# Longformer attention and snake layer on one core: where the next batch's q and k are transposed, when the mask is multiplied in, and which banks hold the scores

## The chip, the cores and the metric

The kernel runs on one core of a Trainium2 chip. The time is device microseconds of one execution; the median of five runs of the kernel before is 370.19 us (369.73 to 371.18). Beside these runs there is one profiled execution, from which all durations below come.

The core has a TensorE (PE in the profile, its weight loads as PEld), a VectorE (DVE), a ScalarE (ACT), a GpSimd (POOL) and a SyncE (SP). Matmuls write to PSUM, which has eight banks of 2 KB per partition; DVE and ACT read them.

## The reference

Two layers follow each other. The first is attention over 8 batches, 8 heads, 576 positions of 64 features, with a window of 32 to both sides and 8 global positions that see and are seen by all. The second is a feed-forward layer over the 4608 tokens with a snake activation.

```python
scores = scale * np.matmul(q, k.transpose(0, 1, 3, 2))
mask = np.abs(pos[:, None] - pos[None, :]) <= window          # window 32
mask = mask | is_global[:, None] | is_global[None, :]
scores = np.where(mask, scores, -1000000000.0)
attn = np.exp(scores - max); attn = attn / (sum + 1e-09)
x = np.matmul(attn, v)        # heads side by side: (4608, 512)
h = x @ w_in                  # (4608, 2048)
s = np.sin(alpha * h)
g = h + s * s / (alpha + 1e-09)
out = g @ w_out               # (4608, 512)
```

## The kernel before, in words

The work is cut into nine phases `p` of a loop at the end of the kernel. Phase `p` (1 to 7) computes the attention of batch `p`, and between its steps it puts the second product of the feed-forward layer (`mm2`) for the 512 tokens of chunk `p-1`. Then it computes the first product and the activation (`mm1`) for chunk `p`. Phase 0 has attention of batch 0 in an order of its own, written out as a string of names; phase 8 has no attention. A chunk needs the batches up to its own number.

The order on every engine is the order in which the program issues instructions (`manual_schedule`). So a line that comes earlier in the text of a step is also earlier in its engine's queue.

**Attention.** Keys and queries of a batch come from memory with positions on partitions (`KS`, `QS`, four transfers of 288 KB, issued by POOL in the first step of the phase before they are used). `stage_T(b, hp)` turns one of four head pairs: 12 transposes of k into the PSUM tile `Kps`, which DVE copies to `kTw[hp]` (L465), and 12 transposes of q into a PSUM tile, which ACT copies to `qT[hp]` (L476). There is one `Kps`, one tile for q at a time, and one `kTw[hp]` and `qT[hp]` for each pair, used by all batches in turn.

The scores are cut into six units `n`. Unit 0 uses pair 0, unit 1 pairs 0 and 1, unit 2 pair 1, unit 3 pair 2, unit 4 pairs 2 and 3, unit 5 pair 3. For a unit, `stage_Q` makes 16 score matmuls into the tile `Sp` (two banks, one buffer, L502), ACT takes the exponential into `E` (L508) and DVE multiplies the mask in (L510). `stage_D` sums over keys with a matmul with ones into `den` (L533); ACT makes 1/sum out of it with a logarithm and an exponential (L539, L541), and DVE sums the global columns (L518, L524). `stage_V` multiplies with the values into `num` (L551), and DVE multiplies with 1/sum into `xT` (L570). `stage_G` (DVE, then eight small POOL copies, L586) writes the global rows of the batch.

`step(j)`, for j from -3 to 5, issues V of unit j, D of unit j+1 and Q, with its mask product, of unit j+3. The function `run` puts `mm2` slots after each step, by the list `counts`. A slot is four matmuls of 128x512; four slots make one output tile of 128 tokens (`ts` 0 to 3), which is then copied to `osb` (L700 on ACT, L698 on DVE for the last tile) and stored. Two slots are issued ahead of step -3. In phases 2 to 7 the third therefore follows step -3, and the fourth, which completes tile 0 and issues its copy, follows step -2.

Pairs 0 and 1 of the next batch are turned in `mm1` (after its slots 10 and 13), pairs 2 and 3 in attention, after steps -2 and 0.

**mm1.** For each of 16 blocks `nt` there are four matmuls into a bank `hb` (L653), a sine on ACT (L660), a square on POOL, ACT or DVE as a table `sq_late` says (L666, L668), and on DVE the sum `H2b = S2 * recip + h` (L643), which frees the bank. That sum is issued two blocks later.

**Banks.** `psC` holds `Kps` and one bank `ops` throughout. The other six banks are `hb` in `mm1` and `num`, `den`, `qp`, `o2`, `Sp` in attention, handed over tile by tile. `Sp` has the two highest banks before the change. The `hb` tiles of `mm1` are given out in the order 2, 7, 6, 5, 4, 3 and then as they come free.

Of the kernel before, what the change touches and what calls it, by code (L numbers as in the profile page):

```python
# [17 lines left out]
def kernel(  # L18
# [11 lines left out]
    nc = tc.nc  # L30
# [442 lines left out]
    def T_Q(b, hp, qpool, qtag, copy):  # L473
        Qps = qpool.tile([P, S], BF, name=qtag)
        T_half(qk[b][0], b, hp, Qps)
        copy(out=qT[hp][:, :, 0:QB], in_=Qps[:].rearrange("p (i c) -> p i c", c=QB))  # L476

    def stage_T(b, hp, pool, tag):
        T_K(b, hp, Kps, nc.vector.tensor_copy)
        T_Q(b, hp, pool, tag, nc.scalar.copy)  # L480

# [15 lines left out]
    def stage_Q(psA, b, n):  # L497
        Sp = psA.tile([P, 2, CH], F32, name="Sp")
        i0 = blocks(n)[0][1]
        for m, (hp, i) in enumerate(blocks(n)):  # L500
            for t, pr in heads:
                nc.tensor.matmul(  # L502
                    out=Sp[:, t, m * QC : (m + 1) * QC],
                    lhsT=kTw[hp][pr, i, :], rhs=qT[hp][pr, i, :],
                    start=True, stop=True, skip_group_check=True,
                )
        E = epool.tile([P, 2, EW], BF, name="E")
        nc.scalar.activation(out=E[:], in_=Sp[:, :, 0:EW], func=AF.Exp, scale=scale)  # L508
        mk = MASK[:, i0 : i0 + NB, :].rearrange("p u c -> p (u c)")
        nc.vector.tensor_tensor(  # L510
            out=E[:], in0=E[:], in1=mk[:, None, :].to_broadcast([P, 2, EW]), op=ALU.mult
        )
        return E

# [78 lines left out]

    def attention(b, psA, t_at=None):


        Es, recs = {}, {}
        gn = gpool.tile([P, 2, NHP, NG], F32, name="gn")
        gd = gpool.tile([P, 2, NHP, NG], F32, name="gd")
        gr = gpool.tile([P, NHP, NG], F32, name="gr")  # L600

        def step(j):
            if j == -3:
                nc.scalar.preload_act_table_set("natural_log_exp_and_others")  # L604
            if j >= 0:
                stage_V(psA, b, j, Es.pop(j), recs.pop(j), gn)
            if 0 <= j + 1 < NUN:
                recs[j + 1] = stage_D(psA, j + 1, Es[j + 1], gd)
                if j + 2 == NUN:
                    stage_Gd(gd, gr)  # L610
                    nc.scalar.preload_act_table_set("trig_and_small")
            if j + 3 < NUN:
                Es[j + 3] = stage_Q(psA, b, j + 3)

        def one(op, j):
            if op == "Q":
                Es[j] = stage_Q(psA, b, j)
            elif op == "D":
                recs[j] = stage_D(psA, j, Es[j], gd)
                if j + 1 == NUN:  # L620
                    stage_Gd(gd, gr)
                    nc.scalar.preload_act_table_set("trig_and_small")
            else:
                stage_V(psA, b, j, Es.pop(j), recs.pop(j), gn)

        if t_at is None:
            return one, partial(stage_G, b, gn, gr)
        parts = [partial(step, j) for j in range(-LEAD, NUN)]
        for hp, j in t_at.items():
            parts[j + LEAD] = partial(chain, parts[j + LEAD], partial(stage_T, b, hp, psA, "qp"))  # L630
        return parts, partial(stage_G, b, gn, gr)

    def chain(*fs):
        for f in fs:
            f()


    def mm1(c, H2b, psB, sq):
# [10 lines left out]
        for nt in range(NT):  # L649
            def slot(nt=nt):  # L650
# [12 lines left out]
                S2 = spool.tile([P, CH], BF, name="S2")  # L663
                eng = sq(nt)
                if eng is nc.scalar:
                    nc.scalar.activation(out=S2[:], in_=Sb[:], func=AF.Square)  # L666
                else:
                    eng.tensor_tensor(out=S2[:], in0=Sb[:], in1=Sb[:], op=ALU.mult)  # L668
# [9 lines left out]
    def mm2(c, H2b, pools, cut=False):  # L678
# [3 lines left out]
        for ts in range(CH // P - (1 if cut else 0)):  # L682
            for g in range(NT // G4):
                def slot(ts=ts, g=g):
# [10 lines left out]
                    if g == NT // G4 - 1:  # L695
                        osb = osbp.tile([P, DM], F32, name="osb")
                        if ts == CH // P - 1:
                            nc.vector.tensor_copy(out=osb[:], in_=ops[:])  # L698
                        else:
                            nc.scalar.copy(out=osb[:], in_=ops[:])  # L700
# [43 lines left out]

    sq_late = lambda nt: {5: nc.scalar, 10: nc.vector, 15: nc.vector}.get(nt, nc.gpsimd)
    sq_last = lambda nt: nc.vector if nt % 4 == 3 or nt > 11 else nc.gpsimd
# [28 lines left out]
    def phase_0():  # L775
        Q, D_, V = (partial(partial, one, o) for o in "QDV")
        fs = {
# [3 lines left out]
        for hp, (kp, ck, qpool, tag) in enumerate(  # L781
            ((Kps, acopy, psA0, "qp"), (Kps0, vcopy, psC, "ops"), (Kps, vcopy, psA0, "qp"), (Kps0, vcopy, psC, "ops"))
        ):
            fs[f"K{hp}"] = partial(T_K, 0, hp, kp, ck)
            fs[f"q{hp}"] = partial(T_Q, 0, hp, qpool, tag, acopy if hp < 3 else vcopy)
            fs[f"G{hp}"] = partial(globals_hp, hp, psA0, "num", vcopy if hp else acopy)
            fs[f"n{hp}"] = partial(globals_in, 1, hp)
        fs["k1"] = partial(globals_hp, 1, psA0, "den", vcopy, (0,))
        fs["p1"] = partial(globals_hp, 1, psA0, "num", vcopy, (1,))
        for o, f in (("Q", Q), ("D", D_), ("V", V)):  # L790
            fs.update({f"{o}{j}": f(j) for j in range(NUN)})
        order = (
            "warm K0 q0 G0 Q0 K1 k1 q1 p1 loads Q1 D0 Q2 D1 K2 q2 G2 D2 Q3 vg K3 q3 G3 D3 Q4 V0 V1 D4 Q5 V2 V3 D5 V4 "
            "alpha V5 last keep A vn kb n0 n1 n2 n3"
# [4 lines left out]
    for p in range(NCH):  # L799
# [4 lines left out]
        elif p < B:  # L804
            with phase_pool("psA", 1) as psA:
                for tag, shape, dt_ in (
                    ("num", [P, NB, QC], F32), ("den", [P, NB, QC], F32),
                    ("qp", [P, S], BF), ("o2", [P, DM], F32),
                ):
                    psA.tile(shape, dt_, name=tag)  # L810
                fill = mm2(p - 1, H2[p - 1], ((psC, "ops"), (psA, "o2")) * 2)
                if p == 1:
                    fill[:8] = [fill[4 * (i % 2) + i // 2] for i in range(8)]
                parts, last = attention(p, psA, {2: -2, 3: 0})
                counts = [1, 1, 1, 1, 1, 2, 2, 1, 0]
                fill.pop(0)()
                fill.pop(0)()
                if p + 1 < B:
# [3 lines left out]
                    for hp in range(NHP):  # L822
                        i_ = hp + LEAD + 1
                        parts[i_] = partial(chain, parts[i_], partial(globals_in, p + 1, hp))
                run(parts + [last], counts + [0], fill)
        else:
# [5 lines left out]
        with phase_pool("psB", 6) as psB:  # L832
# [3 lines left out]
            if p < 3:  # L836
                m1[5] = partial(chain, m1[5], partial(globals_t, p + 1, psB, "hb"))
            if p + 1 < B:
                i_ = (10, 13)
                pre = [partial(shift_v, p + 1), partial(global_v, p + 1)]  # L840
                if p == 0:
                    m1[5] = partial(chain, m1[5], *pre)
                    m1[6] = partial(chain, m1[6], w_loads[3])
                    pre, i_ = (), (12, 14)
                m1[i_[0]] = partial(chain, m1[i_[0]], *pre, partial(stage_T, p + 1, 0, psB, "hb"))
                m1[i_[1]] = partial(chain, m1[i_[1]], partial(stage_T, p + 1, 1, psB, "hb"))
            run(m1, [1, 1, 1, 0] * (NT // 4) if p == B else [0] * NT, fill if p == B else [])
# [33 lines left out]
```

The softmax here doesn't subtract the row's maximum and nothing guards it: scores larger than these inputs give would overflow.

## Time and profile before

| what | value |
|---|---|
| median of five runs | 370.19 us |
| profiled execution, its own time | 369.81 us |
| its span in the profile | 368.0 us |
| PE / DVE / ACT / POOL busy, of the span | 91% / 64% / 67% / 59% |
| from one phase's table load to the next, phases 4 to 7 | 38.18, 38.17, 38.15 us |
| granted PE clock after the first 37 us | 1.00 |

The 1.8 us between the span and the execution's own time lie outside the profile. A phase shows in the profile as a pair of ACT table loads: L604 at the start of attention and L611 near its end. Phases 3 to 7 start within a fraction of a microsecond of the same length, so one of them can be read for all. Times in the timeline are from the start of the span, "idle before" is time in which an engine stood, with the instruction that released it.

### The profile page before, as it was taken

The numbers are of one execution on the slowest core, as the hardware profiler recorded it, in microseconds if no ns is written. First come the engines' busy times: TensorE is split into PE (matmuls) and PEld (weight loads), VectorE is DVE, ScalarE is ACT, GpSimd is POOL, SyncE is SP. The second block draws the span as 40 slices with busy tenths as digits, with TensorE's granted clock in tenths as the row PEclk, the third lists the DMA queues.
The fourth block names the chain that finished last, engine by engine and source line by source line (L and its number), as shares of the span: only waits on it lengthen the run. The fifth ranks groups of instructions, "written<-read, shape, count | busy, mean of one in ns | idle before, by whom it ended". The sixth has DMA issues, their size and how long they took to land.

```text
span 368.0 us, 9350 instructions
## 1 busy us (share of the span) xinstructions
PE 335.9 (91%) x3684; PEld 172.1 (47%) x3738; DVE 234.5 (64%) x511; ACT 248.1 (67%) x378; POOL 217.7 (59%) x316
## 2 busy tenths in 40 slices
PE   5588988999989998999899989998999999999995
PEld 4464444444444444445444454445444544444444
DVE  5565784648763896469746965597649764864610
ACT  3556876768874888487857886678757965845411
POOL 9867798158953895198717881789078005955000
PEclk9557999999999999999999999999999999999999
DMA  9999999941993269642994099509950001001012
GB/s 76 168 197 179 196 175 171 160 117 22 69 175 102 65 39 169 88 109 18 169 110 110 3 160 105 139 0 130 139 137 4 30 30 57 2 0 57 30 66 78
DMA packets 133150, 35.40 MB, mean 96 GB/s; under 512 B 121794, under 2 KB 126818, under 8 KB 133106
## 3 DMA queue, kind: packets, MB, share of 16 engines
q0 software_dynamic: 123120, 20.04, 75.3%
q1 hardware_dynamic: 9682, 14.63, 13.5%
q8 instruction: 29, 0.48, 0.5%
q10 hardware_dynamic: 304, 0.14, 0.1%
q14 instruction: 15, 0.12, 0.1%
HBM read 38.95 MB, written 9.44 MB: 131 GB/s over the span
## 4 chain that ended last, share of the span: by engine, by line
PE 63%; ACT 13%; DVE 7%; DMA 6%; POOL 5%; issue 4%; POOLq 1%; ACTq 0%; DVEq 0%
PE hb L653 27%; PE ops L690 13%; PE o L690 10%; ACT E L508 4%; DMA w_out<-in_moe_w_out_dram 4%; PE num L551 3%; ACT Sb L660 3%; PE Sp L502 2%; ACT L604 2%; DMA QS<-in_q_dram 2%; DVE H2b L643 2%; DVE S L668 2%; DVE kTw L465 2%; PE hb L690 2%; PE Kps L456 2%
## 5 line engine op out<-in xcount | busy, mean ns | idle before, releaser
L660 ACT ACTIVATE Sb<-hb,alphaT 128x512 bf16<-128x512 f32 x144 | 98.1, 686 | 56.5 <-PE hb L653 54.1
L653 PE MATMUL hb<-xT,w_in 128*128 128x512 bf16 x558 | 129.7, 379 | 2.5 <-DVE H2b L643 1.2
L668 POOL TENSOR_TENSOR S<-Sb 128x512 bf16<-128x512 bf16 x108 | 109.7, 1042 | 35.7 <-ACT Sb L660 35.5
L643 DVE SCALAR_TENSOR_TENSOR H2b<-S,recipT,hb 128x512 bf16<-128x512 bf16 x144 | 102.3, 739 | 24.7 <-POOL S L668 24.4
L653 PEld LDWEIGHTS <-w_in 128*128 128x128 bf16 x576 | 55.1, 98 | 66.9 <-issue 2.3
L690 PEld LDWEIGHTS <-H2b 128*128 128x128 bf16 x560 | 49.7, 98 | 57.8 <-issue 4.2
L690 PE MATMUL ops<-w_out,H2b 128*128 128x512 bf16 x283 | 70.7, 380 | 2.2 <-issue 2.1
L690 PE MATMUL o<-w_out,H2b 128*128 128x512 bf16 x209 | 51.0, 380 | 3.5 <-issue 2.4
L510 DVE TENSOR_TENSOR E<-E,MASK 128x896 bf16<-128x896 bf16 x48 | 30.3, 630 | 37.1 <-ACT E L508 36.0
L586 POOL COPY xT<-xg 128x4 bf16 x64 | 13.0, 203 | 65.9 <-DVE xg L584 62.5
L508 ACT ACTIVATE E<-Sp 128x896 bf16<-128x896 f32 x48 | 43.6, 908 | 8.9 <-PE Sp L502 5.7
L539 ACT ACTIVATE lnd<-den 128x384 f32<-128x384 f32 x48 | 23.5, 490 | 24.9 <-PE den L533 23.2
L570 DVE TENSOR_TENSOR xT<-num,rec 128x384 bf16<-128x384 f32 (+1 forms) x60 | 25.8, 450 | 11.3 <-PE num L551 10.9
L502 PE MATMUL Sp<-qT,kTw 64*128 64x56 bf16 x768 | 20.9, 190 | 12.3 <-ACT E L508 4.1
L668 DVE TENSOR_TENSOR S<-Sb 128x512 bf16<-128x512 bf16 x27 | 18.0, 667 | 17.3 <-ACT Sb L660 17.1
L502 PEld LDWEIGHTS <-kTw 64*128 64x128 bf16 x768 | 15.9, 96 | 25.2 <-issue 17.1
L541 ACT ACTIVATE rec<-lnd 128x384 f32<-128x384 f32 x48 | 25.1, 523 | 1.5
L551 PEld LDWEIGHTS <-VW 120*64 120x64 bf16 (+1 forms) x768 | 16.8, 115 | 18.8 <-issue 11.4
L465 DVE COPY kTw<-Kps 128x1344 bf16<-128x1344 bf16 x29 | 24.5, 846 | 0.0
L128 POOL DMA_DIRECT2D KS<-in_k_dram x18 | 20.8, 1153 | 0.6 <-issue 0.6
L551 PE MATMUL num<-E,VW 120*64 120x56 bf16 (+1 forms) x720 | 20.1, 197 | 0.2 <-DVE gn L524 0.2
L128 POOL DMA_DIRECT2D QS<-in_q_dram x18 | 20.2, 1122 | 0.0
(135 smaller groups left out, 298.4 us busy)
## 6 DMA issues: line engine op xcount, KB each, us to landing
out_dram<-osb SPq DMA_DIRECT2D x35, 256.0 KB
KS<-in_k_dram POOLq DMA_DIRECT2D x14, 288.0 KB, 5.7
QS<-in_q_dram POOLq DMA_DIRECT2D x14, 288.0 KB, 12.3
VW<-in_v_dram POOLq DMA_DIRECT2D x12, 336.0 KB, 10.7
VW<-VW SPq DMA_DIRECT2D x7, 384.0 KB
w_in<-in_moe_w_in_dram POOLq DMA_DIRECT2D x2, 1024.0 KB
w_out<-in_moe_w_out_dram POOLq DMA_DIRECT2D x2, 1024.0 KB, 14.9
VW<-VW SPq DMA_DIRECT2D x7, 240.0 KB
```

What stands on the lines that cost most here:

```text
L128: nc.gpsimd.dma_start(out=dst[:, h0 : h0 + nh].rearrange("p h t d -> p (h t) d"), in_=heads_ap(src, b, h0, 0, TW, 0, nh * NTW),)
L465: copy(out=kTw[hp][:, :, 0:KB], in_=bass.AP(tensor=base.tensor, offset=base.offset, ap=[list(base.ap[0]), [QB, NW], [1, KB]],),)
L502: nc.tensor.matmul(out=Sp[:, t, m * QC : (m + 1) * QC], lhsT=kTw[hp][pr, i, :], rhs=qT[hp][pr, i, :], start=True, stop=True, skip_group_ch ...
L508: nc.scalar.activation(out=E[:], in_=Sp[:, :, 0:EW], func=AF.Exp, scale=scale)
L510: nc.vector.tensor_tensor(out=E[:], in0=E[:], in1=mk[:, None, :].to_broadcast([P, 2, EW]), op=ALU.mult)
L551: nc.tensor.matmul(out=num[pr, m, :], lhsT=W[0:nk, i % 2, 2 * hp + t, i // 2, :], rhs=E[0:nk, t, m * QC : (m + 1) * QC], start=b > 0 or m ...
L570: nc.vector.tensor_tensor(out=xT[:, hp, x0 : x0 + nb * QB].rearrange("p (u c) -> p u c", u=nb), in0=num[:, m0 : m0 + nb, 0:QB], in1=rec[:, ...
L643: nc.vector.scalar_tensor_tensor(out=H2b[:, n_, :], in0=s_[:], scalar=recipT[:, n_ : n_ + 1], in1=h_, op0=ALU.mult, op1=ALU.add,)
L653: nc.tensor.matmul(out=h2[:], lhsT=w_in[:, ci, nt * P : (nt + 1) * P], rhs=xT[:, ci, c * CH : (c + 1) * CH], start=(ci == 0), stop=(ci == ...
L660: nc.scalar.activation(out=Sb[:], in_=h2[:], func=AF.Sin, scale=alphaT[:, nt : nt + 1])
L668: eng.tensor_tensor(out=S2[:], in0=Sb[:], in1=Sb[:], op=ALU.mult)
L690: nc.tensor.matmul(out=ops[:], lhsT=H2b[:, nt, ts * P : (ts + 1) * P], rhs=w_out[:, nt, :], start=(nt == 0), stop=(nt == NT - 1),)
```

## The change

- `step` issues the mask product of a unit one step after its scores (new `stage_M`): that of unit 0 in step -1, ahead of D of unit 0; that of unit j+2 in step j, after D of unit j+1.
- Transposes: in phases 2 to 6, all four pairs of the next batch are turned in steps 2 to 5 of the attention, between D and Q; the ACT copy of q is issued after the scores of the step. `mm1` of these phases has none, and phase 7 has none at all. In phase 1, pairs 2 and 3 of batch 1 are turned in steps -2 and -1, pair 0 of batch 2 in step 5, and pairs 1 to 3 in `mm1`, after slots 2, 5 and 8. The transposes and the global keys that are done during `mm1` use the bank `ops` and no longer an `hb` bank.
- `stage_G` moves into step 5, ahead of the last transposes.
- The tiles in attention are laid out in another order: `den`, `Sp`, `num`, `o2`, `qp`.
- `counts` gives one slot after steps -3 to 2, two after steps 3 and 4, four after step 5. In phase 1, the first eight slots are 0, 1, 4, 5, 2, 6, 3, 7.
- The copy of output tile 0 goes from ACT to DVE (`ts % 3 == 0`).
- In `mm1`, blocks 3, 9, 15 are squared on DVE and 5, 12 on ACT (before: 10, 15 and 5), and a pending sum is issued ahead of a square on DVE.

```diff
     def T_Q(b, hp, qpool, qtag, copy):
-        copy(out=qT[hp][:, :, 0:QB], in_=Qps[:].rearrange("p (i c) -> p i c", c=QB))
+        return partial(copy, out=qT[hp][:, :, 0:QB], in_=Qps[:].rearrange("p (i c) -> p i c", c=QB))
...
+    def stage_M(n, E):
+        i0 = blocks(n)[0][1]
         mk = MASK[:, i0 : i0 + NB, :].rearrange("p u c -> p (u c)")
         nc.vector.tensor_tensor(
             out=E[:], in0=E[:], in1=mk[:, None, :].to_broadcast([P, 2, EW]), op=ALU.mult
         )
...
         def step(j):
             if j >= 0:
                 stage_V(psA, b, j, Es.pop(j), recs.pop(j), gn)
+            if j + 1 == 0:
+                stage_M(0, Es[0])
             if 0 <= j + 1 < NUN:
                 recs[j + 1] = stage_D(psA, j + 1, Es[j + 1], gd)
...
+            if 0 < j + 2 < NUN:
+                stage_M(j + 2, Es[j + 2])
+            if j + 1 == NUN:
+                stage_G(b, gn, gr)
+            late = [f() for f in at.get(j, ())]
             if j + 3 < NUN:
                 Es[j + 3] = stage_Q(psA, b, j + 3)
+            chain(*late)
...
                 eng = sq(nt)
+                if eng is nc.vector and len(pend) > 1:
+                    add_out()
...
-                        if ts == CH // P - 1:
+                        if ts % 3 == 0:
                             nc.vector.tensor_copy(out=osb[:], in_=ops[:])
...
-    sq_late = lambda nt: {5: nc.scalar, 10: nc.vector, 15: nc.vector}.get(nt, nc.gpsimd)
+    sq_late = lambda nt: {3: nc.vector, 5: nc.scalar, 9: nc.vector, 12: nc.scalar, 15: nc.vector}.get(nt, nc.gpsimd)
...
-                    ("num", [P, NB, QC], F32), ("den", [P, NB, QC], F32),
-                    ("qp", [P, S], BF), ("o2", [P, DM], F32),
+                    ("den", [P, NB, QC], F32), ("Sp", [P, 2, CH], F32), ("num", [P, NB, QC], F32),
+                    ("o2", [P, DM], F32), ("qp", [P, S], BF),
...
-                    fill[:8] = [fill[4 * (i % 2) + i // 2] for i in range(8)]
-                parts, last = attention(p, psA, {2: -2, 3: 0})
-                counts = [1, 1, 1, 1, 1, 2, 2, 1, 0]
+                    fill[:8] = [fill[i] for i in (0, 1, 4, 5, 2, 6, 3, 7)]
+                if p == 1:
+                    at = {-2: [T_(1, 2)], -1: [T_(1, 3)], 5: [T_(2, 0)]}
+                elif p + 1 < B:
+                    at = {2 + hp: [T_(p + 1, hp)] for hp in range(NHP)}
+                else:
+                    at = {}
+                parts = attention(p, psA, at)
+                counts = [1, 1, 1, 1, 1, 1, 2, 2, 4]
...
-                m1[5] = partial(chain, m1[5], partial(globals_t, p + 1, psB, "hb"))
+                m1[5] = partial(chain, m1[5], partial(globals_t, p + 1, psC, "ops"))
...
-                m1[i_[0]] = partial(chain, m1[i_[0]], *pre, partial(stage_T, p + 1, 0, psB, "hb"))
-                m1[i_[1]] = partial(chain, m1[i_[1]], partial(stage_T, p + 1, 1, psB, "hb"))
+                    if p == 1:
+                        ts = {2: (2, 1), 5: (2, 2), 8: (2, 3)}
+                for i_, (b_, hp) in ts.items():
+                    m1[i_] = partial(chain, m1[i_], partial(both, stage_T, b_, hp, psC, "ops"))
```

## The prediction, made before the changed kernel was run

> **What bounds the kernel now.** I read the page's busy shares first, then the granted clock and the busy times by stage, then the chain of waits for where PE is made to wait, and last the timeline of one whole phase (phase 5, 208.5 to 246.7 us). Page and stages:
>
> ```profile
> PE 335.9 (91%) x3684; PEld 172.1 (47%) x3738; DVE 234.5 (64%) x511; ACT 248.1 (67%) x378; POOL 217.7 (59%) x316
> ...
> core 0: us, PE busy (x) PEld busy (x) DVE busy (x) ACT busy (x) POOL busy (x), PEclk, DMA share, GB/s
> 193.03:209.48 16.45, 16.10 (x115) 7.74 (x116) 12.67 (x17) 12.47 (x20) 12.97 (x13) 1.00 0.25 63
> 209.48:231.20 21.72, 20.13 (x309) 10.37 (x312) 13.56 (x36) 16.23 (x25) 11.79 (x24) 1.00 1.47 124
> ```
>
> The two rows are mm1 and attention of one phase, 38.17 us. PE has 36.2 us of that at full clock, so the phase is PE work plus the gaps that others force on it. The gaps, from the chain of waits:
>
> ```profile
> 215.29 0.81 ACT E L508
> 216.10 0.39 ACT lnd L539
> 216.49 0.02 issue
> 216.51 0.52 ACT rec L541
> 217.04 0.81 ACT E L508
> 217.85 0.02 issue
> 217.87 0.69 DVE E L510
> 218.56 0.78 DVE kTw L465
> 219.34 0.05 issue
> 219.38 0.28 PE Sp L502 x8
> ```
>
> In these 4 us the chain leaves PE: exponentials, a mask product and the key copy end in the second half of the scores of unit 4. The timeline gives the sizes:
>
> ```profile
> 206.13 0.45 PE L456 MATMUL Kps<-identb,KS 96*64 96x96 bf16 x12 [0.25 <-DVE kTw L465]
> ...
> 209.86 2.05 DVE L643 SCALAR_TENSOR_TENSOR H2b<-S,recipT,hb 128x512 bf16<-128x512 bf16 x3
> ...
> 211.83 0.61 DVE L510 TENSOR_TENSOR E<-E,MASK 128x896 bf16<-128x896 bf16 x1
> ...
> 213.65 0.38 PE L533 MATMUL den<-E,ones 120*64 120x448 bf16 x2
> 213.76 0.59 ACT L700 COPY osb<-ops 128x512 f32<-128x512 f32 x1 [0.15 <-PE ops L690]
> ...
> 216.15 0.38 PE L502 MATMUL Sp<-qT,kTw 64*128 64x56 bf16 x16 [0.27 <-ACT E L508]
> ...
> 219.38 0.28 PE L502 MATMUL Sp<-qT,kTw 64*128 64x56 bf16 x8 [0.48 <-DVE kTw L465]
> ```
>
> By start to start, PE loses 0.25 us at the second transpose in mm1, 0.32 at the scores of unit 3 (D before it began at 215.52 and takes 0.31) and 0.60 at those of unit 4 (first half began at 218.63, takes 0.155): 1.17 us. The mask product of unit 0 at 211.83 came at once behind the last sum of mm1, and D at 213.65 did not wait for it.
>
> **What the skill says.** The Trainium skill, "PSUM — Partial Sum Buffer", section "Engine vs sequencer instructions", has the ScalarE, VectorE and GpSimd queues as strict FIFO and matmuls in program order. The trace agrees: DVE's instructions stand in the order of the program throughout this phase. My main step rests on that. "SBUF — State Buffer", "Who interferes with whom", says that a `tensor_tensor` with both inputs in SBUF contends with GpSimd's reads. The trace fits: the DVE square of block 10 took 1.28 us (203.38) beside POOL's squares, that of block 15 0.44 us (209.49) with POOL idle. "ScalarE: Activation LUTs", "What ACT_TABLE_LOAD costs", gives 1283 ns and a drain of 1380 ns; the load here takes 1.28 us, and the exponential starts 0.01 us after it, so no drain is charged.
>
> **The change part by part**, first for phases 2 to 6.
>
> *Transposes.* A pair is 24 transposes, 0.64 us of PE with the return to matmuls (216.46 to about 217.10), wherever it lies; four pairs before, four after. Away from mm1 go the 0.25 us wait and about 0.1 us for each change from an mm1 matmul to a transpose (the first transpose of a phase comes 0.1 after the matmuls end), 0.2 us. In attention the scores of unit 4 no longer follow a key copy: 0.60 goes. With no q copy and no output copy on ACT ahead of them, the exponentials of units 2 and 3 come sooner: 0.32 goes. Removed: 0.25 + 0.20 + 0.60 + 0.32 = 1.37 us.
> The loads cover the new place. POOL issues the four q and k loads of the next batch at 209.59 to 213.15, ahead of the values; they take the median 5.7 (k) and 7.2 us (q) in this trace, so the last lands about 220.4. Step 2 begins at 220.56 now, and the pairs of the second quads come only in step 4. The key and query tiles are free by then: the last scores of pair 0 are unit 1's, of pair 2 unit 4's. Late steps have DVE room: 1.5 us idle before the multiplication at 226.2 against 0.85 for a key copy. So the copies are hidden; without that cover each costs up to 0.85.
>
> *Output copy of tile 0 on DVE, mask product a step later.* These two meet. The fourth slot of mm2 follows step -2 and issues the copy into DVE's queue. The mask product of unit 0 is now issued in step -1, behind it, and D of unit 0 waits for that product. So after the fourth slot's last matmul: 0.16 to the copy (mm1 of the next phase begins at 231.07, the copy of tile 3 at 231.23), 0.64 until DVE takes the next instruction (it lasts 0.69), 0.62 for the mask product, 0.05 to PE: 1.47 us, where 0.08 is the usual change. PE loses 1.4 us. Queued behind the waiting D on PE are the scores of unit 2, the next slot and V of unit 0, so nothing fills the gap; ACT, done with exponential 1, stands too.
> After it, exponential 2 follows D by 0.38 + 0.05 + 0.5 (L539) + 0.45 (L541) + 0.85 = 2.25 us, and PE reaches the scores of unit 3 after D 0.31, Q 0.31, slot 0.86, V 0.28, D 0.31 and 0.1 of change = 2.17: a wait of about 0.13. Later mask products have a step of slack.
>
> *mm1.* ACT's new square of block 12 puts the last sine about 0.1 late (0.63 us of backlog, worked off at 0.17 us a block), and so the first exponential: 0.1. DVE's new squares at blocks 3 and 9 share with POOL: 2 x about 1.1 us, against one such and two key copies (1.7) before. The sums still keep within six banks: nothing. Limits: -0.2 (POOL gets relief) to +0.7 (the sum of block 15 comes late for the fourth slot, which needs it; it ended 3.4 us after the first slot's start, and the slot will be reached at about 3.6).
> *Banks.* `Sp` in banks given up by blocks 10 and 11: the first scores were not waiting before (210.33, at once behind eight matmuls), so nothing.
>
> Sum for one phase: +1.40 + 0.13 + 0.10 - 1.37 = +0.26 us; five phases, +1.3.
>
> *Phase 7* has no transposes in mm1 on either side, and those of its attention moved into phase 6's. Removed: 0.32 and 0.53 us of score waits (292.48, 295.65). Added: 1.63. Its mm1 waited 0.22 us for a bank (319.79), because the sum of block 8 stood behind the square of block 10; the new order removes that. +0.56.
>
> *Phases 0 and 1.* PE waits 1.09 us for bank `o2` at 54.55; gone, but the second half of w_out lands at 59.56 and its first user starts at 59.61, so nothing is gained before that.
>
> ```profile
> 44.68 14.88 DMA w_out<-in_moe_w_out_dram
> ...
> 63.55 0.21 PE L456 MATMUL qp<-identb,QS 96*64 96x96 bf16 x1 [0.47 <-issue]
> ```
>
> Afterwards the unit 4 wait (0.7) goes. The q transposes of pair 3 took from 61.82 to 63.70, 1.5 us over their 0.33, under "issue": an unexplained stall while DMA is full. It may stay or go; I take half, 0.75, less 0.15 for the scores. -1.3. In mm1 there are three pairs for two: 0.64 + 0.1. Pair 2 follows the global keys in the one bank `ops`: their DVE copy ran at 84.39 to 84.61, 1.3 us after they ended (83.28), as it queues behind a sum; the q transposes would want the bank at 83.56. A wait of 1.1. The phase: +0.55.
>
> Sum: 1.3 + 0.56 + 0.55 = +2.4 us. On the profiled execution's 369.81 (368.0 of span, 1.8 around it) that is 372.2; on the median of 370.19, 372.6.
>
> **Rivals.**
> *The gaps that go are larger than I can name.* Per phase, PE's matmuls start to start sum to 128 x 0.2155 = 27.6, attention 6 x 0.9 = 5.4, transposes 2.3: 35.3 of 38.17. The 2.9 us are 1.4 named (with 0.23 at the scores of unit 1) and 1.5 of small changes. If transposes at the end, away from score handovers, also halve the small ones, a phase wins 0.75 - 0.26 = 0.5; if DVE finds the copy's bank ready earlier and half of the 1.4 vanishes, 0.7 more. Six phases at -1.0 or so and the phase 1 stall gone entirely (-0.75): 365 us. For it: ACT is relieved in the early steps. Against: the queue order is certain, and PE has nothing to do meanwhile.
> *A wash.* The stall of phase 1 goes, the wait for `ops` is short, and D's wait is just paid: 370.2.
> *DVE falls behind in mm1.* The sum of block 15 ends 0.7 late, the fourth slot waits, and copy, mask product and D shift with it. 6 x 0.6 more: 376. It decides once DVE needs over 0.2 us more per mm1 than now. DVE's squares cost 1.28 and not 0.44 wherever POOL works, which speaks for it; no key copies there, against it.
>
> **How the numbers follow.** What a measurement here can tell from no change is about 0.3%, 1.1 us. My forecast, 372.6, has chance 0.45, own range 370.6 to 374.6 (0.36 slower, 0.09 same). The larger gain 0.32, all faster. The wash 0.10 (0.07 same, 0.03 faster). DVE behind 0.13, slower. So faster 0.35, same 0.16, slower 0.49. The low end must cut into the larger gain: 365.0 to 376.0 leaves about 0.2 out.
>
> **What would show it.** In the changed profile: D (ones times E) of unit 0 idle about 1.4 us in phases 2 to 7, released by the mask product, with the DVE copy of tile 0 just ahead; no wait of scores for a key copy; mm1 at about 14 us in phases 2 to 7; in phase 1 q transposes waiting for the copy of the global keys. I am wrong if D's wait is under 0.7 us, or if the phases from table load to table load come under 37.7 us.

## The result, and the profile after

The changed kernel takes 368.92 us (median of 28 runs) beside 370.11 us of the kernel before on the same chip (49 runs): a ratio of 0.9973, 95% interval 0.996 to 0.9986. It is slightly faster; the forecast was 2.4 us slower. The profiled execution took 368.98 us, with a span of 367.0 us against 368.0.

The stages, cut at the first matmul of `mm1` and at the first slot of `mm2` in each phase, in both timelines:

| stage | before | after | difference | forecast |
|---|---|---|---|---|
| up to `mm1` of phase 0 | 36.02 | 36.12 | +0.10 | 0 |
| phase 0, `mm1` | 16.41 | 15.80 | -0.61 | 0 |
| phase 1, attention / `mm1` | 25.33 / 15.61 | 24.04 / 16.80 | -1.29 / +1.19 | -1.3 / +1.84 |
| phase 2, together | 38.70 | 40.20 | +1.50 | +0.26 |
| phases 3 to 6, together | 152.76 | 152.84 | +0.08 | +1.04 |
| phase 7, attention / `mm1` up to phase 8's slot | 22.49 / 15.96 | 21.99 / 15.00 | -0.50 / -0.96 | +0.78 / -0.22 |
| the rest | 44.74 | 44.23 | -0.51 | 0 |
| sum | 368.03 | 367.04 | -1.0 | +2.4 |

The busy times by stage, first of the changed kernel, for phase 5 and phase 7 (attention of phase 5 with the `mm1` ahead of it, attention and `mm1` of phase 7):

```profile
core 0: us, PE busy (x) PEld busy (x) DVE busy (x) ACT busy (x) POOL busy (x), PEclk, DMA share, GB/s
195.66:209.47 13.81, 13.76 (x65) 6.27 (x64) 10.27 (x16) 10.85 (x17) 9.47 (x10) 1.00 0.29 74
209.47:233.83 24.36, 21.96 (x360) 12.07 (x364) 16.43 (x40) 17.77 (x28) 13.29 (x25) 1.00 1.31 112
285.81:307.80 21.99, 19.85 (x265) 9.75 (x268) 13.18 (x36) 15.53 (x24) 3.32 (x10) 1.00 0.10 38
307.80:322.81 15.01, 14.57 (x68) 6.65 (x69) 11.13 (x17) 11.81 (x18) 10.76 (x11) 1.00 0.05 18
```

And of the kernel before, phase 5 (attention, and the `mm1` ahead of it) and phase 7:

```profile
208.51:231.07 22.56, 20.97 (x313) 10.77 (x317) 14.52 (x38) 16.95 (x27) 12.65 (x24) 1.00 1.41 120
192.90:208.51 15.61, 15.26 (x111) 7.34 (x112) 11.71 (x16) 11.75 (x18) 12.10 (x12) 1.00 0.26 66
284.84:307.33 22.49, 20.96 (x313) 10.77 (x317) 14.46 (x38) 16.92 (x27) 2.66 (x9) 1.00 0.10 36
307.33:323.29 15.96, 14.89 (x68) 6.64 (x69) 11.94 (x17) 11.41 (x17) 13.24 (x13) 1.00 0.05 17
```

Together the two stages have the length that they had, 38.17 us: `mm1` went from 15.61 to 13.81, attention from 22.56 to 24.36. In `mm1` PE now works all but 0.05 us; in attention it stands for 2.4 us where it stood for 1.6. Phase 7 lost 48 of its 313 matmul records, the two pairs of transposes, and 1.1 us of PE time with them.

Of the chain of waits before, the 4 us of exponentials and key copy at units 3 and 4 are gone. In their place the changed kernel's chain of waits has this (start, duration, what):

```profile
212.70 0.38 PE Sp L501 x16
213.08 0.98 PE ops L705 x4
214.06 0.02 issue
214.09 0.69 DVE osb L713
214.78 0.68 DVE E L513
215.46 0.04 issue
215.50 0.40 PE den L535 x2
215.89 0.02 issue
215.91 0.50 ACT lnd L541
```

PE ends the fourth slot, DVE copies its output, then multiplies the mask into unit 0, and only then D runs. The waits on PE, in total, times and longest, show that this is the one large new wait: 0.37 us of the 8.7 are in phase 0, the other six are the phases 2 to 7, with 1.31 us in phases 2, 3 and 7 and 1.45 or 1.46 in 4 to 6. No wait of scores for a key copy is left in the list.

```profile
PE den L535 <- DVE E L513: 8.7, 7, 1.5
...
PE ops L705 <- DMA w_out<-in_moe_w_out_dram: 1.1, 1, 1.1
...
PE ops L456 <- DVE GT L430: 0.4, 1, 0.4
...
PE hb L666 <- DVE H2b L656: 0.4, 1, 0.4
```

Phase 7's `mm1` is where 0.96 us were found that the forecast did not have. The timeline of the kernel before there:

```profile
317.80 1.28 DVE L668 TENSOR_TENSOR S<-Sb 128x512 bf16<-128x512 bf16 x1 [0.21 <-ACT Sb L660]
318.76 4.22 POOL L668 TENSOR_TENSOR S<-Sb 128x512 bf16<-128x512 bf16 x4
...
319.79 1.89 PE L653 MATMUL hb<-xT,w_in 128*128 128x512 bf16 x8 [0.22 <-DVE H2b L643]
...
322.43 1.02 PE L653 MATMUL hb<-xT,w_in 128*128 128x512 bf16 x3 [0.75 <-DVE H2b L643]
```

And that of the changed kernel:

```profile
317.98 0.58 DVE L683 TENSOR_TENSOR S<-Sb 128x512 bf16<-128x512 bf16 x1
...
318.32 2.13 POOL L683 TENSOR_TENSOR S<-Sb 128x512 bf16<-128x512 bf16 x2
...
321.95 1.02 PE L666 MATMUL hb<-xT,w_in 128*128 128x512 bf16 x4 [0.39 <-DVE H2b L656]
```

PE waited for two sums before, 0.22 and 0.75 us, and waits for one of 0.39 after. That is 0.58 of the 0.96 us; the rest is in gaps that the list does not name. The DVE square that stands in the way of the sums takes 0.58 and not 1.28 us. In both it ends about 0.3 us after the POOL square that is running (319.08 after 318.76; 318.56 after 318.32). Taken instruction by instruction this holds in all 13 traces: 246 DVE squares began while POOL had 0.16 to 1.00 us of a square left, and each ended 0.28 to 0.30 us after it; those that met none took 0.41 to 0.57 us. What differs is how much of POOL's square was left when DVE began: about 1.0 us before, 0.3 after. A sum now goes first (317.31 to 318.06, while the sine that the square needs was ready at 317.38). The new blocks and the new order of the sum were never run apart, so how the gain divides between them is not shown.

### The profile page after: what moved, and what is told of

Same layout as the page of the kernel before. It is cut to its first block, busy times and chain, and to the rows that moved or that the text cites. A ratio compares the mean times of both kernels' runs of the same rounds, so it can differ in the third digit from the quotient of the medians.

```text
span 367.0 us, 9353 instructions
## 1 busy us (share of the span) xinstructions
PE 334.6 (91%) x3684; PEld 173.5 (47%) x3738; DVE 237.9 (65%) x527; ACT 245.8 (67%) x376; POOL 203.9 (56%) x302
## 4 chain that ended last, share of the span: by engine, by line
PE 62%; ACT 13%; DMA 9%; DVE 6%; issue 4%; POOL 4%; POOLq 1%; ACTq 0%; DVEq 0%
PE hb L666 27%; PE ops L705 11%; PE o L705 11%; DMA w_out<-in_moe_w_out_dram 4%; ACT E L507 4%; PE num L553 3%; DMA VW<-in_v_dram 3%; DVE H2b L656 3%; PE Sp L501 3%; PE den L535 2%; DMA QS<-in_q_dram 2%; ACT L607 2%; PE hb L705 2%; ACT L616 2%; ACT Sb L673 2%
## 5 line engine op out<-in xcount | busy, mean ns | idle before, releaser
L673 ACT ACTIVATE Sb<-hb,alphaT 128x512 bf16<-128x512 f32 x144 | 96.9, 684 | 57.9 <-PE hb L666 54.4
L666 PE MATMUL hb<-xT,w_in 128*128 128x512 bf16 x564 | 128.0, 379 | 1.2 <-DVE H2b L656 0.4
L683 POOL TENSOR_TENSOR S<-Sb 128x512 bf16<-128x512 bf16 x94 | 96.0, 1041 | 48.5 <-ACT Sb L673 44.1
L705 PE MATMUL ops<-w_out,H2b 128*128 128x512 bf16 x283 | 71.6, 380 | 2.2 <-DMA w_out<-in_moe_w_out_dram 1.1
L501 PE MATMUL Sp<-qT,kTw 64*128 64x56 bf16 x768 | 19.9, 189 | 8.8 <-ACT E L507 4.1
L535 PE MATMUL den<-E,ones 120*64 120x448 bf16 x96 | 19.4, 385 | 9.3 <-DVE E L513 8.7
```

The source lines that it names most:

```text
L501: nc.tensor.matmul(out=Sp[:, t, m * QC : (m + 1) * QC], lhsT=kTw[hp][pr, i, :], rhs=qT[hp][pr, i, :], start=True, stop=True, skip_group_ch ...
L535: nc.tensor.matmul(out=den[pr].rearrange("p u c -> p (u c)"), lhsT=ones[0 : KB + NG], rhs=E[0 : KB + NG, t, :], start=True, stop=True, ski ...
L666: nc.tensor.matmul(out=h2[:], lhsT=w_in[:, ci, nt * P : (nt + 1) * P], rhs=xT[:, ci, c * CH : (c + 1) * CH], start=(ci == 0), stop=(ci == ...
L673: nc.scalar.activation(out=Sb[:], in_=h2[:], func=AF.Sin, scale=alphaT[:, nt : nt + 1])
L705: nc.tensor.matmul(out=ops[:], lhsT=H2b[:, nt, ts * P : (ts + 1) * P], rhs=w_out[:, nt, :], start=(nt == 0), stop=(nt == NT - 1),)
```

## The experiments

All kernels compute the whole of the reference. Times are compared with the kernel before on the same chip, whose median there is 367.15 to 367.53 us; ratios carry 95% intervals. The changed kernel's 0.9973 is from the first chip. Two theories stood against each other. **Theory A**: D's wait is a real loss of about 1.4 us a phase that nothing repays, and the changed kernel would be clearly faster without it. **Theory B**: the wait only takes slack that another wait would have taken, and what the change won or lost is elsewhere, in `mm1`.

**The wait of D, taken away in three ways.** First, the copy of output tile 0 goes back to ACT:

```diff
-                        if ts % 3 == 0:
+                        if ts == CH // P - 1:
```

> The changed kernel with the copy of output tile 0 back on ACT (tile 3 alone on DVE). Theory A, the wait of D for the mask product of unit 0 (1.45 us in phases 2 to 7 of the changed kernel) is a real loss that is not paid back later: D of unit 0 waits under 0.3 us, a phase is about 1.2 us shorter, six phases 7 us, so about 362 us. Theory B, the wait only uses up time that the exponentials on ACT would take anyway: the wait moves to the scores of units 2 to 4, and the time stays between 367.5 and 369.5 us.

360.13 us, ratio 0.9814 (0.978 to 0.9847). Second, the copy stays on DVE, but the mask product of unit 0 is issued ahead of it, at the end of step -2:

```diff
-            if j + 1 == 0:
-                stage_M(0, Es[0])
...
                 Es[j + 3] = stage_Q(psA, b, j + 3)
+            if j + 2 == 0:
+                stage_M(0, Es[0])
             chain(*late)
```

> The changed kernel with the mask product of unit 0 alone issued at the end of step -2, ahead of the copy of tile 0, which stays on DVE. Theory A: as with the copy on ACT, D no longer waits for DVE, about 362 us; ACT is spared the copy, so up to 1 us better than with the copy there. Theory B: 367.5 to 369.5 us.

360.26 us, ratio 0.9794 (0.9762 to 0.9826). Its timeline, phase 5:

```profile
208.38 0.61 DVE L513 TENSOR_TENSOR E<-E,MASK 128x896 bf16<-128x896 bf16 x1
...
208.69 1.04 PE L705 MATMUL ops<-w_out,H2b 128*128 128x512 bf16 x4
...
209.66 0.38 PE L535 MATMUL den<-E,ones 120*64 120x448 bf16 x2
209.77 0.69 DVE L713 COPY osb<-ops 128x512 f32<-128x512 f32 x1 [0.78 <-PE ops L705]
```

The same two DVE instructions in the other order: D follows 0.97 us after the start of the fourth slot instead of 2.49 (213.01 to 215.50), and the copy runs beside it. The phase is 36.70 us, 1.47 shorter. Third, all mask products go back to the step of their scores:

```diff
-            if j + 1 == 0:
-                stage_M(0, Es[0])
...
-            if 0 < j + 2 < NUN:
-                stage_M(j + 2, Es[j + 2])
...
                 Es[j + 3] = stage_Q(psA, b, j + 3)
+                stage_M(j + 3, Es[j + 3])
```

> The changed kernel with every mask product issued with its scores again (no step later), the copy of tile 0 on DVE. If only the first mask product matters: the same as with that one early, about 362 us under theory A. If the later step of the others helps too (the sums over global columns and the multiplication into xT come ahead of the mask on DVE): 1 to 3 us slower than that. Theory B: 367.5 to 369.5 us.

360.35 us, ratio 0.9802 (0.9761 to 0.9842). Three edits with only the wait in common win the same: theory A holds, and the move of one line makes a version that is about 2% faster than the kernel before. That the other mask products lie a step later wins nothing that shows here, nor does the copy on DVE in place of ACT. By the ratios to the kernel before, which are from different chips, the three win 1.6 to 1.8% on the changed kernel, where the six waits, 8.3 us, would be 2.2%. In phases 5 and 6 each of the three gains 1.34 to 1.48 us. Some of what is missing is in phase 4, whose attention takes 24.28, 24.54 and 23.71 us in these three and 23.02, 22.89 and 22.88 in phase 5; the last section shows such a stall.

**The part in `mm1`.** The kernel before, with the new table of squares and the sum ahead of a DVE square:

```diff
                 eng = sq(nt)
+                if eng is nc.vector and len(pend) > 1:
+                    add_out()
...
-    sq_late = lambda nt: {5: nc.scalar, 10: nc.vector, 15: nc.vector}.get(nt, nc.gpsimd)
+    sq_late = lambda nt: {3: nc.vector, 5: nc.scalar, 9: nc.vector, 12: nc.scalar, 15: nc.vector}.get(nt, nc.gpsimd)
```

> The kernel before with the new split of the squares and with the pending sum ahead of a square on DVE; nothing else. My part by part sum gives the bank waits of phase 7 and the handover to phase 8 (0.22 and 0.75 us in the profile of before) and the wait for the key copy in mm1 (0.25 us a phase) as the most it can win: 368.2 to 370, about 369.3 us. Rival, that this part is what made the changed kernel faster: under 368.5 us.

365.39 us, ratio 0.9944 (0.9924 to 0.9965): 2.1 us of 367.53, where the forecast had 0.22 us in phase 7 and nothing elsewhere. The `mm1` stages of its trace give 2.4 us: 0.33 in each of phases 3 to 6, 0.96 in phase 7, and 0.04 in each of phases 1 and 2. The reverse, the changed kernel with the old squares and without that order:

```diff
                 eng = sq(nt)
-                if eng is nc.vector and len(pend) > 1:
-                    add_out()
...
-    sq_late = lambda nt: {3: nc.vector, 5: nc.scalar, 9: nc.vector, 12: nc.scalar, 15: nc.vector}.get(nt, nc.gpsimd)
+    sq_late = lambda nt: {5: nc.scalar, 10: nc.vector, 15: nc.vector}.get(nt, nc.gpsimd)
```

> The changed kernel with the old split of the squares and without the sum ahead of a square on DVE. Theory C, the gain of 1 us of the change comes from this part and the rest of it costs: about 2.1 us slower than the changed kernel (the 0.9944 that this part gave alone), a ratio to before of 1.002 to 1.004. Rival, the part matters in the kernel before only, where the key copies stood in mm1 as well: within 0.7 us of the changed kernel, a ratio of 0.997 to 0.999.

371.94 us, ratio 1.0111 (1.0063 to 1.0159): with the old `mm1` the changed kernel is slower than the kernel before. The busy times by stage (`mm1` of one phase, then that of phase 7) of the kernel before with the new `mm1`:

```profile
191.35:206.63 15.28, 15.28 (x113) 7.22 (x112) 11.88 (x18) 12.20 (x19) 10.31 (x10) 1.00 0.27 68
304.82:319.82 15.00, 14.83 (x70) 6.65 (x68) 11.13 (x17) 11.81 (x18) 10.76 (x11) 1.00 0.05 19
```

and of the changed kernel with the old one:

```profile
199.15:213.33 14.18, 13.96 (x65) 6.24 (x64) 10.29 (x14) 10.69 (x16) 11.77 (x12) 1.00 0.29 72
312.14:328.09 15.95, 14.99 (x69) 6.60 (x68) 11.94 (x17) 11.40 (x17) 13.23 (x13) 1.00 0.05 17
```

The new squares, with the order of the sum that belongs to them, are worth 0.33 (15.61 to 15.28) and 0.38 us (14.19 to 13.81) in each of phases 3 to 6, and in both pairs phase 7 goes with them: 15.95 with the old, 15.00 with the new. Its 0.96 us are theirs alone. This kernel loses 1.4% or 5 us on the changed one, of which 4 x 0.38 + 0.95 and 0.2 in phases 1 and 2 are named so, 2.7 in all. For the rest, the profile shows phase 2, whose attention takes 29.50 us against 26.10 (in an execution of 374.91 us, 3 over the median). That is a stop of PE with a halved clock after it, which is taken up at the end; how many of the other executions have it is not known.

**The banks.** The kernel with the early mask product of unit 0, and the old layout:

```diff
-                    ("den", [P, NB, QC], F32), ("Sp", [P, 2, CH], F32), ("num", [P, NB, QC], F32),
-                    ("o2", [P, DM], F32), ("qp", [P, S], BF),
+                    ("num", [P, NB, QC], F32), ("den", [P, NB, QC], F32),
+                    ("qp", [P, S], BF), ("o2", [P, DM], F32), ("Sp", [P, 2, CH], F32),
```

> The kernel with the early mask product of unit 0 and the tiles in the old order of banks, scores last. My prediction put the bank order at nothing. If that holds: 360 us, a ratio of 0.979 to 0.981. Theory D, with the transposes out of the hb banks, blocks 13 and 14 fall into the last two banks and the first scores wait for the sum of block 14: 0.8 us later first scores and first exponential in each of 6 or 7 phases, about 365 us, a ratio of 0.992 to 0.996.

364.28 us, ratio 0.9917 (0.989 to 0.9944): 4.0 us slower than with the new layout (4.5 by the ratios). Its waits on PE begin with

```profile
PE Sp L501 <- DVE H2b L656: 4.9, 6, 0.8
```

so the first scores of each phase wait 0.8 us for a sum of `mm1` to free the bank. In phase 5 it is the first of the last two sums, that of block 14:

```profile
210.40 1.39 DVE L656 SCALAR_TENSOR_TENSOR H2b<-S,recipT,hb 128x512 bf16<-128x512 bf16 x2
...
211.19 0.38 PE L501 MATMUL Sp<-qT,kTw 64*128 64x56 bf16 x16 [0.81 <-DVE H2b L656]
```

DVE is not later here: that sum ends 2.65 us after the first slot of `mm2` (211.14 after 208.49), and 2.74 after it in the kernel before. There the first scores began 1.82 us after the slot, ahead of the end of all three last sums, so the same two banks were held by earlier blocks. This fits what was expected of this kernel: the transposes no longer take `hb` banks, which shifts the order in which the blocks get them. The version with two parts at once, further below, agrees: it has the old layout and the new squares, but its transposes in `hb` banks, and its first scores do not wait. The forecast looked at the kernel before, where nothing waited, and put it at nothing.

**The place of the transposes.** The early mask product again, with the transposes at their old places (pairs 0 and 1 in `mm1`, 2 and 3 in steps -2 and 0), but still issued ahead of the scores of their step:

```diff
-                    at = {2 + hp: [T_(p + 1, hp)] for hp in range(NHP)}
...
+                at = {-2: [T_(p, 2)], 0: [T_(p, 3)]}
...
-                        ts = {2: (2, 1), 5: (2, 2), 8: (2, 3)}
+                    ts = {10: (p + 1, 0), 13: (p + 1, 1)}
```

> The kernel with the early mask product of unit 0 and the transposes back in their old steps and mm1 slots (in the bank ops in mm1). My prediction counts 1.37 us a phase for moving them (waits of unit 3 and 4 scores, of the second transpose, and changes on PE) in phases 2 to 7, less 0.74 us and a wait in phase 1: about 6 us slower than with the late transposes, 366 us, a ratio of 0.993 to 0.998. Rival, the place of the transposes is worth little and the rest of the change does it: under 363 us.

360.29 us, ratio 0.9781 (0.9744 to 0.9817), the same as with the late places within the intervals; a phase takes 21.48 + 15.28 = 36.76 us against 36.70. So the late steps themselves win nothing that shows. The reverse, the kernel before with only the order within the step changed (transposes ahead of the scores, the q copy after the exponential):

```diff
+            late = [stage_T(b, hp, psA, "qp") for hp, j_ in t_at.items() if j_ == j] if t_at else []
...
                 Es[j + 3] = stage_Q(psA, b, j + 3)
+            chain(*late)
...
-        for hp, j in t_at.items():
-            parts[j + LEAD] = partial(chain, parts[j + LEAD], partial(stage_T, b, hp, psA, "qp"))
```

> The kernel before with one thing moved: in steps -2 and 0 the two transposes come ahead of the scores of the step, not behind them, and the ACT copy of q behind the exponential; all else as before, the old squares too. Theory E, the waits of the scores of units 3 and 4 (0.32 and 0.60 us a phase) came from the order inside the step, the key copy behind the mask product on DVE and the q copy ahead of the next exponential, and not from the place of the transposes: a phase is 0.9 to 1.2 us shorter, about 361 us on the chip of the last runs (before 367.2), a ratio of 0.981 to 0.986. Rival, it takes the mask a step later or the new squares as well: above 0.993.

363.34 us, ratio 0.9893 (0.9867 to 0.9919): the sign as expected, the size less. Attention of a phase goes from 22.56 to 21.94 us. Its timeline at the scores of units 3 and 4, which before lost 0.32 and 0.60 us:

```profile
210.81 0.42 PE L456 MATMUL Kps<-identb,KS 96*64 96x96 bf16 x12
211.07 0.42 PE L456 MATMUL qp<-identb,QS 96*64 96x96 bf16 x12
211.64 0.38 PE L502 MATMUL Sp<-qT,kTw 64*128 64x56 bf16 x16
...
213.19 0.36 PE L533 MATMUL den<-E,ones 120*64 120x448 bf16 x2
213.48 0.70 PE L502 MATMUL Sp<-qT,kTw 64*128 64x56 bf16 x16
```

The transposes fill part of the time for which the scores of unit 3 would wait: from the transposes of q to the scores it is 0.57 us, where 0.38 is usual, so 0.19 is left. Those of unit 4 are no longer cut in two by a released wait, though they last 0.70 where 0.38 is usual: that 0.32 is left of the 0.60. With the 0.23 us that the scores of unit 1 lost before and do not lose here, this is about the 0.62 us.

**Masks a step later, alone.** The kernel before with only this part (`stage_M` split off `stage_Q` as in the change):

```diff
+            if j + 1 == 0:
+                stage_M(0, Es[0])
...
+            if 0 < j + 2 < NUN:
+                stage_M(j + 2, Es[j + 2])
```

> The kernel before with the mask products a step later and nothing else; the copy of output tile 0 stays on ACT. Theory E: the key copy of step 0 no longer stands behind a mask product on DVE, so the 0.60 us wait of unit 4 goes and the 0.32 us of unit 3 stays; D of unit 0 waits under 0.4 us: a ratio of 0.988 to 0.994. If deferring costs by itself (D late for its mask): 1.000 or more.

364.92 us, ratio 0.9936 (0.991 to 0.9961); attention 22.20 us. Here, too, the key copy is no longer behind a mask product, and the wait of unit 4 is gone. The 0.32 us of unit 3, which was expected to stay, is 0.14. D of unit 0 waits only 0.26 us for its mask product, ahead of which DVE has a key copy (208.54 to 209.31) and no output copy, which in this kernel is ACT's.

**The bank of the global keys**, in an `hb` bank again, with the early mask product:

```diff
-                m1[5] = partial(chain, m1[5], partial(globals_t, p + 1, psC, "ops"))
+                m1[5] = partial(chain, m1[5], partial(globals_t, p + 1, psB, "hb"))
```

> The kernel with the early mask product of unit 0 and the transposes of the global keys back in an hb bank. In the profile of the changed kernel the q transposes of pair 2 wait 0.40 us for the copy of the global keys in phase 1, where I had predicted 1.1: without that sharing mm1 of phase 1 is 0.4 to 0.7 us shorter (16.8 to about 16.3), which the total can just not show: 359.5 to 360.5 us. If the sharing costs nothing or another bank is waited for instead: 16.7 or more.

359.82 us, ratio 0.9779 (0.9748 to 0.9811). `mm1` of phase 1 takes 16.20 us in place of 16.80, but the whole cannot be told from the other versions.

**Two parts of the change at once** in the kernel before, the order within the step and the new `mm1`, by the two diffs above.

> The same with the new squares and the sum ahead of a square on DVE. If the two parts add up (0.9944 alone for the second): a ratio of 0.975 to 0.981, the same as the kernel with everything and the early mask product (0.979), so that late transposes, deferred masks, new banks and new counts are not needed for the gain. Rival, the deferral or the new counts carry part of it: 0.985 or more.

360.71 us, ratio 0.9811 (0.9789 to 0.9833), beside the product of the two single ones, 0.9893 x 0.9944 = 0.9838. The two gains add, within the intervals. This version keeps all transposes in the steps and slots where they were, and its time cannot be told from that of the changed kernel without D's wait. In the profile, though, a full phase of it takes 21.86 + 15.29 = 37.15 us, where the two kernels with the early mask product take 36.70 and 36.76; so the deferred masks, the counts, the copy and the layout together may be worth another 0.4 us a phase, which the totals do not show.

## Why the prediction was wrong, point by point

**D's wait: right, in place, size and cause.** Forecast 1.47 us with 0.08 usual, seen 1.31 to 1.46 in phases 2 to 7; taken away by three edits, the time falls by about 6 us (from 0.9973 to about 0.980 of the kernel before). The rival of larger gains, which let half of this wait vanish, fell with it. Of the two small terms beside it, the wait of unit 3's scores is there (0.14 us at 217.81, for 0.13 forecast; the terms as listed sum to 2.23 and not 2.25 us, 0.06 over the 2.17 of PE, so the agreement is in part luck), and the late sine costs nothing: unit 1's scores start 3.23 us after the first slot in both kernels.

**Phase 7: the step that failed first, a term left out of the sum.** The forecast had "Removed: 0.32 and 0.53 us of score waits. Added: 1.63" for its attention, +0.78. It wrote in the same paragraph that the transposes of its attention had moved into phase 6, and did not take off their time, two pairs at 0.64. With these 1.28 the sum is -0.50; measured is -0.50, and PE lost 48 matmuls and 1.1 us of busy time there. This was a slip of the sum, not of the mechanism; that it agrees to the hundredth is chance, since D waited 1.31 and the sine cost nothing. The same count missed one pair that attention of phase 1 gained (0.64, pair 0 of batch 2), so that the phase's -1.29 holds more gain than the forecast named: about 1.9 us.

**mm1: the step that failed second.** "The sums still keep within six banks: nothing", with limits of -0.2 to +0.7 a phase. The runs showed a gain of 2.1 us alone, 0.33 to 0.38 in each of phases 3 to 6 and 0.96 in phase 7. Two things were missed. DVE's squares were priced by the one row of 1.28 us, though they cost what is left of POOL's square plus 0.3, and a sum issued ahead lets that shrink. The row of 0.44 us that was read as one "with POOL idle" obeys the same rule: the POOL square before it runs from 208.61 to 209.65, so 0.16 us of it were left at 209.49. This fits what the Trainium skill, "SBUF — State Buffer", "Who interferes with whom", says of a DVE instruction with two SBUF inputs beside a GpSimd one that reads SBUF. The same section says that the order of issue decides which of the two is held up; in all 246 cases it is DVE's square, begun second, that ends later. And the wait at the end of phase 7, 0.75 us for a bank, stood in the profile before and was not read: only the 0.22 us one ahead of it was.

**Phases 2 to 6: near in sum, wrong in its parts.** The forecast gave +0.26 a phase, measured 0.00 in phases 5 and 6. In `mm1` it took off 1.28 for two pairs and 0.45 for the second transpose's wait and the changes, 1.73 in all; measured is 1.80 in phases 3 to 6. But the pairs' wait and changes were only 0.14 (15.61 to 14.19 with the old squares is 1.42), and the squares the other 0.38: two errors that cancel, by luck. In attention it had +1.99 (two pairs more 1.28, D 1.40, unit 3's wait 0.13, sine 0.10, less 0.92); measured is +1.80. The 0.92 us at the scores of units 3 and 4 did go, but not because the transposes went to late steps. In the version with the transposes at their old places 0.08 us of it is left (unit 4's scores take 0.46 for 0.38). In the kernel before, the order within the step alone removes 0.41 of it, and the mask a step later alone 0.78. The q loads were given 7.2 us, the median of three between 205 and 250 us (that of the whole trace is 12.3); no transpose of phases 2 to 6 waited for one.

**Banks: "nothing" was wrong.** The new layout is worth 4 us once the transposes have left the `hb` banks. It does not show in the difference of the two kernels, since it keeps a wait from arising.

**Phase 1.** The wait for `ops` came (0.40 us, released by the copy of the global keys) and not as 1.1: DVE made the copy 0.5 us after the global keys were turned, behind a sum that was nearly done, where before another sum, itself waiting for POOL, stood ahead of it. That attention came out at -1.29 for -1.3 is luck. The stall of 1.5 us, of which half was booked, is not seen at all. The 0.7 us of unit 4, which were to go, did not: its scores now wait 0.71 us for an exponential. And the pair that was not charged is paid for by pair 3 of batch 1, which is now turned before w_out has landed, where PE has to wait in any case (1.11 us at 59.46).

**The rival on the slow side** did not come: the last sum of `mm1` ends at 212.78 in phase 5, 3.31 us after the first slot, and the fourth slot did not wait.

**Neither sign of being wrong** that the forecast named (a wait under 0.7 us, phases under 37.7 us) appeared, and the changed kernel was faster all the same. They looked at phases 2 to 6 alone, where the forecast was close. By the table, 3.4 us lie between forecast and measurement: 2.0 in phase 7 (1.28 in attention, 0.74 in `mm1`), 1.0 in the start, `mm1` of phase 0 and the end together, 1.0 in phases 3 to 6 and 0.6 in phase 1, less 1.2 in phase 2, which took longer than forecast. The 0.61 us of phase 0 have no cause that is shown. Its squares have a table of their own, which the change leaves as it was; of the new squares only the order of the sum applies there. In the 13 traces the kernels with this order take 15.57 to 17.40 us in this stage, and those without it 16.04 to 16.41. The 0.51 us at the end is mostly the landing of the last store.

## What to carry to other kernels

When work moves between stages, count what each stage holds before and after, for every stage, the last too, before any wait is priced. An instruction put into an in-order queue is late by whatever was issued ahead of it: here one line, moved ahead of a copy, was worth 1.8%, where the version gains 2.1% in all. A layout that changes nothing today can be what lets another edit count; test it in the kernel with that edit.

## What the runs showed of the hardware that was not expected

PE stops inside runs of small matmuls at places where no instruction is awaited, for 0.4 to 2.3 us: 14 times over 0.4 us in the 13 traces, after the first 36 us. In the timeline of the changed kernel with the old squares, phase 2:

```profile
104.98 0.20 PE L501 MATMUL Sp<-qT,kTw 64*128 64x56 bf16 x2
107.53 0.51 PE L501 MATMUL Sp<-qT,kTw 64*128 64x56 bf16 x14 [2.34 <-issue]
107.97 1.89 PE L703 MATMUL o<-w_out,H2b 128*128 128x512 bf16 x4
```

and in that of the kernel with the early mask product, phase 4:

```profile
179.16 0.41 PE L553 MATMUL num<-E,VW 120*64 120x56 bf16 x14
...
181.09 0.22 PE L553 MATMUL num<-E,VW 120*64 120x56 bf16 x2 [1.52 <-issue]
```

A group of 16 equal matmuls is broken after 2 or 14. After the 2.34 us four large matmuls take 1.89 us instead of 1.04. The busy times show why (the third number from the end is the granted PE clock):

```profile
107.53:113.72 6.19, 6.19 (x65) 3.10 (x66) 2.21 (x5) 3.60 (x6) 0.48 (x2) 0.50 1.27 119
```

The clock was 0.50 from 106.89 to 113.72 us and 1.00 on both sides. At half the clock these 6.19 us hold what takes 3.1 at the full one (an estimate), and with the stop of 2.34 that is about the 5.3 us by which the attention of this phase (29.50) exceeds that of the next (24.24). The kernel with the global keys in `hb` has the same in phase 4: a stop of 1.71 us, the clock at 0.50 from 182.56 to 185.98, and 26.38 us of attention where phase 5 has 22.93. After the 1.52 us above, the clock stayed at 1.00, and so it did at every wait of D in the changed kernel, up to 1.46. In four kernels (the one with the transposes at their old places, the one with the global keys in `hb`, and the kernel before with the new `mm1` and with two parts at once) PE waits 1.54 to 2.53 us for w_out near 60 us, and 3.41 us at 0.50 begin within 1.4 us of the end of this wait; five others wait there 1.47 to 1.79 us and keep the full clock. What decides between them is not shown. The profiled executions of the kernel before and of the changed kernel have 1.00 throughout after 37 us, so none of this is in their difference.

The changed kernel has 0.50 us of such a stop at 107.14, which with smaller ones around it is part of its +1.5 in phase 2. In ten of the 14 stops, all those outside the kernel before, PE goes on 2.4 to 2.8 us after one packet of 16 KB started on the instruction queue, while the value, query and key loads filled the DMA engines. The reverse does not hold: each trace has 29 such packets, and most of them bring no stop, also during the loads. The view of the transfers of the first of these kernels, from 103 to 110 us, shows that packet as q8 (queue, kind, packets, MB, share of the engines):

```profile
q0 software_dynamic: 8381, 1.06, 239.7%
q1 hardware_dynamic: 20, 0.03, 1.3%
q8 instruction: 1, 0.02, 0.9%
```

That PE then waits for its own instructions is a guess from this coincidence; no run tried it, and it stays open. The stalls move with the program, and differ by some 2 us between kernels: versions that differ by less than that, as those at 360 us do, are not ranked here.
